# Second weights in two sets, four staging tiles, streamed token operands and PSUM banks by chain in a fused attention and mixture kernel

## The chip, the cores and the metric

The kernel runs on one core of one Trainium2 chip. The time is device microseconds of one execution. Below, PE is TensorE (matrix products), PEld its weight loads, DVE VectorE, ACT ScalarE, POOL GpSimd, and SP the SyncE queue, which issues every transfer of this kernel, in its own order.

## What is computed

First a linear attention with 4 batches, 8 heads, 576 rows and head size 64. Then its output, x of 2304 tokens by 512, goes through 8 experts. Every token visits every expert, and the weights P of the experts are balanced by eight rounds of normalising rows and columns.

```python
logits = x @ w_gate
P = np.exp(logits - logits.max())
for _ in range(8):
    P /= P.sum(1, keepdims=True) + 1e-09
    P /= P.sum(0, keepdims=True) + 1e-09
    P *= N / E
out = np.zeros((N, D), dtype=np.float32)
for e in range(E):
    h = np.maximum(x @ w1[e], 0.0)     # w1[e]: 512 x 1024
    ye = h @ w2[e]                     # w2[e]: 1024 x 512
    out += P[:, e:e + 1] * ye
```

## The kernel before

The attention takes the first 0.2 ms. The rest, some 1.45 ms, is the expert part, and the change lies there.

**Units and steps.** The work of the experts is cut into 16 units: 8 experts, each in two halves of 512 hidden columns (`units`). In each unit the 2304 tokens go by in three chunks of 768 (`CT`, `NCH`), and the second product of a unit is done in 9 steps of two token tiles each (`NP`, `steps`). A step `s` is a unit `u` and a place `n` from 0 to 8 in it. The scheduler that places the instructions of each engine works on a list of 144 steps. It may move an instruction ahead of its place in the program as far as its data and its buffers allow.

**Seven products for eight.** Both matrix products are cut into 2 x 2 blocks and done by seven block products, in the order `ORDER = [1, 5, 6, 3, 7, 2, 4]`, with sums of blocks on either side. Each operand is split into a high and a low part (`wh`, `wl` for weights; `ah`, `al`, `sh`, `sl`, `bh`, `bl` for the left side), and a block product is three products of parts, each in two pieces: six matmuls. `first(u, c, i, g)` does the first layer (banks `hx`, `hz`; 6 matmuls of 384 columns, 42 such groups in a unit), `second(s, i)` the second one (6 matmuls of 256 columns, 63 such groups in a unit). `left_operands_a` and `left_operands_b` make the left sides of a step on DVE and ACT.

**Chains of the second product.** The seven products of a step are summed in three PSUM banks that `bank(name)` hands out: chain x takes 1, 6, 7, 4, chain z takes 5 and 3, and w takes 2. After each product DVE adds the bank into the output tiles (line 660). The next product of the same chain writes on into the same bank, so PE waits at it until DVE has read. Before, x, z, w and the small matmuls of the balancing share four banks of one pool, and whichever is free is handed out.

**Weights.** `stage(u, w)` loads a weight block of a unit as two tiles `st` of 512 KB, out of three staging buffers. `split(u, w, i)` makes the operand of product i: POOL adds or subtracts blocks (line 193; for the second weights in place, in `st`), ACT casts the high part `wh` (line 223), DVE makes the low part `wl` (line 224). First weights have 7 buffers of each part, one set. Second weights have 7 + `W2X` = 11.

**Token operands.** The seven sums of token blocks of each chunk are made once, at the end of the attention, and written to DRAM (`xdram`). In each unit `load_next` brings them back into one of `XSB = 4` buffers `xs`, in the order of use, one load each time a buffer comes free. The operand of product 1 is an exception (`RES = (1,)`): it is loaded once for each chunk into a tile `xr` that stays.

Of the kernel before, what the change touches and what calls it, by code (L numbers as in the profile page):

```python
# [9 lines left out]
F32 = mybir.dt.float32  # L10
# [6 lines left out]
def raw(ap):  # L17

    return ap.bitcast(F32)
# [3 lines left out]
def moe_attention_kernel(  # L23
# [29 lines left out]
    P = 128  # L53
# [3 lines left out]
    SM = JM * P  # L57
    SR = S - SM
    XSB = 4
    RES = (1,)  # L60
    W2X = 4
    FB = 4
    NFB = FF // P // FB
    CT = 6
# [3 lines left out]
    HD = DM // 2  # L68
# [5 lines left out]
    wp = ctx.enter_context(tc.tile_pool(name="wp", bufs=1, side="right"))  # L74
    ps_cm = tc.tile_pool(name="ps", bufs=6, space=bass.MemoryType.PSUM)
    ps = [ps_cm.__enter__()]
    kv_cm = tc.tile_pool(name="ps_kv", bufs=2, space=bass.MemoryType.PSUM, side="right")
    ps_kv = kv_cm.__enter__()

    def bank(name):  # L80
        return ps[0].tile([P, 512], F32, tag="b", name=name)


    ident = const.tile([P, P], F32, name="ident")
# [4 lines left out]


    ORDER = [1, 5, 6, 3, 7, 2, 4]
    xdram = {}

    def token_tile():
# [2 lines left out]
    def token_operands(c, x):  # L97
# [11 lines left out]

        for i in ORDER:  # L110
            if i == 5:
# [61 lines left out]
    wst, wt = {}, {}  # L173
    tmp = {}

    def stage(u, w):
        e, fb = units[u]
        f0 = fb * FB * P
        for r in range(2):
            wst[u, w, r] = t = wp.tile([P, 2, 2, HD], F32, tag="st", bufs=3, name="st")  # L180
            if w == 1:
                src = w1[e][r * HD : (r + 1) * HD, f0 : f0 + FB * P]
            else:
                src = w2[e][f0 + r * HD : f0 + (r + 1) * HD, :]
            nc.sync.dma_start(out=t.rearrange("p k h c -> p k (h c)"), in_=src.rearrange("(k p) c -> p k c", p=P))

    def split(u, w, i):

        def q(r, h):
            return wst[u, w, r][:, :, 1 - h if w == 1 else h]  # L190

        def tt(o, a, b, op=ALU.subtract):
            nc.gpsimd.tensor_tensor(o, a, b, op=op)  # L193


        if w == 1:

            if i == 5:
                tmp[u] = wp.tile([P, 2, HD], F32, tag="t", bufs=1, name="t")
                tt(tmp[u], q(0, 1), q(1, 1), ALU.add)  # L200
            elif i == 6:
                tt(tmp[u], tmp[u], q(0, 0))
            elif i == 3:
                tt(tmp[u], q(1, 0), tmp[u])
            elif i == 7:
                tt(q(0, 1), q(0, 0), q(0, 1))
            o = {1: q(0, 0), 7: q(0, 1), 2: q(1, 0), 4: q(1, 1)}[i] if i not in (5, 6, 3) else tmp[u]
        else:

            if i == 5:  # L210
                tt(q(0, 0), q(0, 1), q(0, 0))
            elif i == 6:
                tt(q(0, 0), q(0, 0), q(1, 1))
            elif i == 7:
                tt(q(0, 1), q(1, 1), q(0, 1))
            elif i == 4:
                tt(q(0, 0), q(1, 0), q(0, 0), ALU.add)
            o = {3: q(1, 1), 7: q(0, 1), 2: q(1, 0)}.get(i, q(0, 0))
        pool = wp if w == 1 else op_
        bufs = 7 + W2X * (w == 2)  # L220
        hi = pool.tile([P, 2, HD], F32R, tag=f"w{w}h", bufs=bufs, name="wh")
        lo = pool.tile([P, 2, HD], F32R, tag=f"w{w}l", bufs=bufs, name="wl")
        nc.scalar.copy(hi, o)  # L223
        (nc.vector if u > 0 or (w == 2 and i in (1, 6, 7, 4)) else nc.gpsimd).tensor_tensor(lo, o, raw(hi), op=ALU.subtract)  # L224
        wt[u, w, i] = (hi, lo)
# [18 lines left out]
    for i in range(2):  # L244
        r, cl = slice(i * D, (i + 1) * D), slice(i * M, (i + 1) * M)
# [253 lines left out]


    outt = {}
    hp_, px, pz = [], [], []
    NP = CT // 2 * NCH
    steps = [(u, n) for u in range(len(units)) for n in range(NP)]
    def order(u):

        return [NCH - 1] + list(range(NCH - 1)) if u == 0 else list(range(NCH))

    chunks = [(u, c) for u in range(len(units)) for c in order(u)]
    hraw, hneg, ops, xop, xres, hacc = {}, {}, {}, {}, {}, {}  # L510
    loads = [(u, c, i) for u, c in chunks[1:] for i in ORDER]

    def load_next():

        while loads:
            u, c, i = loads.pop(0)
            if i in RES:
                if (c, i) not in xres:
                    xres[c, i] = op_.tile([P, 2, 2, HL], F32R, name=f"xr{c}_{i}")
                    nc.sync.dma_start(out=raw(xres[c, i]), in_=xdram[c, i])  # L520
                xop[u, c, i] = xres[c, i]
                continue
            xop[u, c, i] = token_tile()
            nc.sync.dma_start(out=raw(xop[u, c, i]), in_=xdram[c, i])
            return

    def first(u, c, i, g):
# [38 lines left out]
        if g == 1 or both is None:  # L566
# [5 lines left out]
            else:  # L572
                nc.scalar.copy(o, src)  # L573
        if g == 1 and (u, c) != chunks[0] and i not in RES:
            load_next()

    def tiles_of(u, n):

        c, j = order(u)[n // (CT // 2)], n % (CT // 2)
        return [CT * c + j, CT * c + j + CT // 2]  # L580
# [90 lines left out]

    pieces = [(u, c, i, g) for u, c in chunks for i in ORDER for g in range(2)]

# [56 lines left out]
    for i, jb in enumerate(jobs):  # L730
# [4 lines left out]
        if i >= 8 and i % 2 == 0 and (i - 8) // 2 < 7:  # L735
            split(0, 1, ORDER[(i - 8) // 2])
        if i == 24:
# [14 lines left out]
    left_operands_b(0)  # L752
    sc_cm.__exit__(None, None, None)
    ps_cm.__exit__(None, None, None)
    ps[0] = ctx.enter_context(tc.tile_pool(name="ps4", bufs=4, space=bass.MemoryType.PSUM))
    pz.append(ctx.enter_context(tc.tile_pool(name="pz", bufs=1, space=bass.MemoryType.PSUM)))
    op_ = ctx.enter_context(tc.tile_pool(name="op", bufs=1, reuse_waits="tile"))
    for _ in range(XSB):
        load_next()
    for i in ORDER:  # L760
        split(0, 2, i)
# [3 lines left out]
    for s, (u, n) in enumerate(steps):  # L765
        c = n // (CT // 2)
        more = u + 1 < len(units)
        if u == NFB:
            for t in tiles_of(u, n):
                nc.vector.tensor_scalar_mul(outt[t], outt[t], prob[:, t, 0:1])  # L770
        if more:
            if n == 1:
                stage(u + 1, 1)
            if n == 2:
                split(u + 1, 1, ORDER[0])
            if n == NP - 2 - W2X:
                stage(u + 1, 2)
            if NP - 1 - W2X <= n < NP - 1:
                split(u + 1, 2, ORDER[n - (NP - 1 - W2X)])
        for k, i in enumerate(ORDER):  # L780
            second(s, i)
            if n == NP - 1 and more and k + W2X < len(ORDER):
                split(u + 1, 2, ORDER[k + W2X])
            if k < (5, 5, 4)[n % 3] and todo:
                pc = todo.pop(0)
                first(*pc)
                j = ORDER.index(pc[2])
                if pc[1] == order(pc[0])[-1] and pc[3] == 1 and pc[0] + 1 < len(units) and j + 1 < len(ORDER):
                    split(pc[0] + 1, 1, ORDER[j + 1])
            if i == 7 and s + 1 < len(steps):  # L790
                left_operands_a(s + 1)
            if k in (1, 4):
                next(gate, None)
        if s + 1 < len(steps):
            left_operands_b(s + 1)
        if s == NFB * NP - 1:
            for _ in gate:
                pass
        if u == len(units) - 1:
            for t in tiles_of(u, n):  # L800
                store(t)
        ops.pop(s)
# [28 lines left out]
```

## Time and profile before

| | us |
|---|---|
| three runs, median (lowest, highest) | 1668.83 (1668.63, 1671.46) |
| profiled execution, its own time | 1676.44 |
| its span, first to last instruction | 1674.7 |
| PE busy in the span | 1626.8 |
| DVE busy | 1430.5 |
| ACT busy | 783.6 |
| POOL busy | 250.1 |

The profiled execution is 7.6 us longer than the median. PE is busy nearly throughout, but its matmuls overlap, and the end of each is modelled; how fast PE goes is seen from the starts of its instructions, not from the busy share. A wait of DVE, ACT or POOL costs nothing unless PE comes to need what it delays.

### The profile page before, as it was taken

The numbers are of one execution on the slowest core, as the hardware profiler recorded it, in microseconds if no ns is written. First come the engines' busy times: TensorE is split into PE (matmuls) and PEld (weight loads), VectorE is DVE, ScalarE is ACT, GpSimd is POOL, SyncE is SP. The second block draws the span as 40 slices with busy tenths as digits, with TensorE's granted clock in tenths as the row PEclk, the third lists the DMA queues.
The fourth block names the chain that finished last, engine by engine and source line by source line (L and its number), as shares of the span: only waits on it lengthen the run. The fifth ranks groups of instructions, "written<-read, shape, count | busy, mean of one in ns | idle before, by whom it ended". The sixth has DMA issues, their size and how long they took to land.

```text
span 1674.7 us, 29917 instructions
## 1 busy us (share of the span) xinstructions
PE 1626.8 (97%) x11610; PEld 1601.4 (96%) x11610; DVE 1430.5 (85%) x2903; ACT 783.6 (47%) x1408; POOL 250.1 (15%) x232
## 2 busy tenths in 40 slices
PE   7999989999999999999999999999999999999998
PEld 7899889999999999999999999999999999999997
DVE  7999788898978888898888887888889888888878
ACT  6777645443344344443444443434444344444432
POOL 7531131110111011010101010101101010101000
PEclk9999999999999999999999999999999999999999
DMA  9422575554554555556555454555564654555452
GB/s 242 119 80 99 218 284 190 196 194 159 169 177 159 195 175 176 195 162 209 177 175 188 163 187 163 176 189 183 166 206 157 205 185 162 189 159 194 159 189 76
DMA packets 96347, 295.08 MB, mean 176 GB/s; under 512 B 13776, under 2 KB 38352, under 8 KB 96208
## 3 DMA queue, kind: packets, MB, share of 16 engines
q1 hardware_dynamic: 96208, 293.19, 53.0%
q8 instruction: 92, 1.51, 0.4%
q14 instruction: 47, 0.39, 0.1%
HBM read 271.93 MB, written 21.23 MB: 175 GB/s over the span
## 4 chain that ended last, share of the span: by engine, by line
PE 73%; DVE 16%; DMA 5%; issue 2%; ACT 2%; POOL 1%; SPq 0%; ACTq 0%; DVEq 0%
PE hx L554 20%; PE x L640 19%; PE hz L554 13%; PE z L640 10%; DMA st<-in_moe_w_dram 5%; PE w L640 5%; DVE sm L591 3%; DVE wl L224 2%; DVE out L660 2%; DVE hr L571 1%; PE np L433 1%; DVE mx L347 1%; POOL st L193 1%; ACT wh L223 1%; DVE bl L591 1%
## 5 line engine op out<-in xcount | busy, mean ns | idle before, releaser
L554 PE MATMUL hx<-xs,wh 128*128 128x384 f32 x1160 | 279.9, 336 | 0.8 <-ACT hr L573 0.5
L554 PE MATMUL hz<-xs,wh 128*128 128x384 f32 x1152 | 278.3, 336 | 0.0
L660 DVE SCALAR_TENSOR_TENSOR out<-x,prob,out 128x256 f32<-128x256 f32 x504 | 237.8, 476 | 22.9 <-PE x L640 22.8
L554 PEld LDWEIGHTS hx<-xs,wh 128*128 128x128 f32 x1160 | 204.1, 188 | 1.4 <-ACT hr L573 0.9
L554 PEld LDWEIGHTS hz<-xs,wh 128*128 128x128 f32 x1152 | 203.2, 188 | 0.1
L622 ACT ACTIVATE bh<-hr 128x512 fp32r<-128x512 f32 x144 | 91.1, 633 | 233.0 <-PE x L640 188.1
L223 ACT CAST wh<-st 128x512 fp32r<-128x512 f32 x176 | 106.7, 618 | 194.9 <-POOL st L193 80.1
L224 DVE TENSOR_TENSOR wl<-st,wh 128x512 fp32r<-128x512 f32 x169 | 135.1, 802 | 67.2 <-ACT wh L223 66.3
L660 DVE SCALAR_TENSOR_TENSOR out<-z,prob,out 128x256 f32<-128x256 f32 x252 | 120.1, 476 | 83.2 <-PE z L640 83.0
L591 DVE SCALAR_TENSOR_TENSOR sm<-hr,sm 128x256 f32<-128x256 f32 x288 | 147.8, 513 | 3.9
L554 PE MATMUL hx<-xs,wl 128*128 128x384 f32 x580 | 150.8, 336 | 0.0
L554 PE MATMUL hz<-xs,wl 128*128 128x384 f32 x576 | 149.7, 335 | 0.0
L193 POOL TENSOR_TENSOR st<-st 128x512 f32<-128x512 f32 x80 | 106.7, 1342 | 231.1 <-DMA st<-in_moe_w_dram 177.0
L618 ACT CAST sh<-sm 128x512 fp32r<-128x512 f32 x144 | 89.6, 622 | 99.7 <-PE z L640 75.6
L640 PE MATMUL z<-wh,sh 128*128 128x256 f32 x576 | 117.4, 284 | 13.0 <-DVE out L660 12.2
L640 PE MATMUL x<-wh,sh 128*128 128x256 f32 x576 | 118.9, 288 | 2.7 <-ACT wh L223 1.3
L640 PE MATMUL z<-wl,sh 128*128 128x256 f32 x576 | 119.6, 282 | 0.8 <-POOL wl L224 0.8
L640 PE MATMUL x<-wl,sh 128*128 128x256 f32 x576 | 117.0, 281 | 0.0
L640 PE MATMUL z<-wh,sl 128*128 128x256 f32 x576 | 115.1, 281 | 1.8 <-DVE sl L606 1.8
L640 PE MATMUL x<-wh,sl 128*128 128x256 f32 x576 | 115.4, 281 | 0.0
L591 DVE SCALAR_TENSOR_TENSOR bl<-hr,bh 128x512 fp32r<-128x512 f32 x144 | 112.9, 784 | 0.0
L193 POOL TENSOR_TENSOR t<-st 128x512 f32<-128x512 f32 x16 | 21.2, 1322 | 608.4 <-DMA st<-in_moe_w_dram 527.3
(153 smaller groups left out, 3968.4 us busy)
## 6 DMA issues: line engine op xcount, KB each, us to landing
xs<-xd SPq DMA_DIRECT2D x282, 768.0 KB, 4.4
st<-in_moe_w_dram SPq DMA_DIRECT2D x64, 512.0 KB, 5.7
xd<-xs SPq DMA_DIRECT2D x21, 768.0 KB, 4.2
k<-in_k_dram SPq DMA_DIRECT2D x8, 512.0 KB, 6.7
v<-in_v_dram SPq DMA_DIRECT2D x8, 512.0 KB, 5.6
q<-in_q_dram SPq DMA_DIRECT2D x8, 512.0 KB, 6.5
out_dram<-out SPq DMA_DIRECT2D x16, 256.0 KB, 2.3
xr<-xd SPq DMA_DIRECT2D x3, 768.0 KB, 11.5
```

What stands on the lines that cost most here:

```text
L193: nc.gpsimd.tensor_tensor(o, a, b, op=op)
L223: nc.scalar.copy(hi, o)
L224: (nc.vector if u > 0 or (w == 2 and i in (1, 6, 7, 4)) else nc.gpsimd).tensor_tensor(lo, o, raw(hi), op=ALU.subtract)
L347: nc.vector.reduce_max(mx, p3, axis=AX.X)
L433: nc.tensor.matmul(n3[:, i, :], lhsT=qt[g][:, i, :], rhs=kvs[key[0]][:, h, :], start=True, stop=True)
L554: nc.tensor.matmul(pb, lhsT=a[:, k, g * P : (g + 1) * P], rhs=x[:, b, k, :], start=i in (1, 5, 2) and j == 0, stop=j == len(prods) - 1, sk ...
L571: nc.vector.tensor_tensor(o, src, o, op=ALU.add)
L591: nc.vector.scalar_tensor_tensor(o, in0=a, scalar=0.0, in1=b, op0=ALU.max, op1=op)
L618: nc.scalar.copy(sh, sm)
L622: nc.scalar.activation(bh, a[:, 1:], AF.Relu)
L640: nc.tensor.matmul(pb, lhsT=ops[s][i][a][:, f], rhs=wt[u, 2, i][b][:, f], start=bool(start) and j == 0, stop=j == len(prods) - 1, skip_gro ...
L660: nc.vector.scalar_tensor_tensor(o, in0=pb, scalar=prob[:, t, e : e + 1], in1=o, op0=ALU.mult, op1=ALU.add)
```

## The change

- `RES` becomes empty: the operand of product 1 is streamed like the other six, 21 loads of a unit where there were 18, and the three `xr` tiles and their loads are gone.
- The second weights have 14 buffers of each part, two sets (`bufs = 7 * w`). Both staging calls stand at the start of a unit (n = 1 and n = 2), and the seven splits of the second weights stand at places listed in `W2AT`.
- Four staging buffers `st` where there were three.
- Once the expert part has begun, `bank` gives chain x two banks of its own, z one, and w one, which it shares with the balancing. It is four banks as before.

```diff
-    RES = (1,)
-    W2X = 4
+    RES = ()
+    pz = []
     def bank(name):
-        return ps[0].tile([P, 512], F32, tag="b", name=name)
+        if not pz:
+            return ps[0].tile([P, 512], F32, tag="b", name=name)
+        tag = name if name in "xz" else "w"
+        return ps[0].tile([P, 512], F32, tag=tag, bufs=2 if tag == "x" else 1, name=name)
+    W2AT = [(5, 2), (6, 0), (6, 3), (7, 0), (7, 3), (8, 0), (8, 3)]
-            wst[u, w, r] = t = wp.tile([P, 2, 2, HD], F32, tag="st", bufs=3, name="st")
+            wst[u, w, r] = t = wp.tile([P, 2, 2, HD], F32, tag="st", bufs=4, name="st")
-        bufs = 7 + W2X * (w == 2)
+        bufs = 7 * w
-    hp_, px, pz = [], [], []
+    hp_, px = [], []
-    ps[0] = ctx.enter_context(tc.tile_pool(name="ps4", bufs=4, space=bass.MemoryType.PSUM))
+    ps[0] = ctx.enter_context(tc.tile_pool(name="ps4", bufs=1, space=bass.MemoryType.PSUM))
                 split(u + 1, 1, ORDER[0])
-            if n == NP - 2 - W2X:
+            if n == 2:
                 stage(u + 1, 2)
-            if NP - 1 - W2X <= n < NP - 1:
-                split(u + 1, 2, ORDER[n - (NP - 1 - W2X)])
         for k, i in enumerate(ORDER):
             second(s, i)
-            if n == NP - 1 and more and k + W2X < len(ORDER):
-                split(u + 1, 2, ORDER[k + W2X])
+            if more and (n, k) in W2AT:
+                split(u + 1, 2, ORDER[W2AT.index((n, k))])
```

What stands on the engines is set by the scheduler. Three places show it. The first is SP's queue. Before, in the middle of unit 5, it holds the second tile of the second weights for unit 6 (`st_8956`) and the first tile of the first weights for unit 7 (`st_9785`):

```order
L524 DMA xs_9098<-xd2_4_3079 128x1536
L524 DMA xs_9133<-xd0_5_1826 128x1536
L524 DMA xs_9167<-xd0_6_1908 128x1536
L185 DMA st_8956<-in_moe_w2_dram 128x2x512
L524 DMA xs_9244<-xd0_3_1986 128x1536
L524 DMA xs_9279<-xd0_7_2076 128x1536
L524 DMA xs_9388<-xd0_2_2158 128x1536
L185 DMA st_9785<-in_moe_w1_dram 128x2x512
L524 DMA xs_9458<-xd0_4_2238 128x1536
```

Now both tiles of the second weights for unit 6 (`st_8874`, `st_8876`) stand in the middle of unit 4:

```order
L532 DMA xs_8094<-xd0_1_1733 128x1536
L532 DMA xs_8128<-xd0_5_1826 128x1536
L193 DMA st_8874<-in_moe_w2_dram 128x2x512
L532 DMA xs_8200<-xd0_6_1908 128x1536
L532 DMA xs_8239<-xd0_3_1986 128x1536
L193 DMA st_8876<-in_moe_w2_dram 128x2x512
L532 DMA xs_8320<-xd0_7_2076 128x1536
```

So these loads moved ahead by a whole unit, and loads of operand 1 (`xd0_1`) came into the queue.

The second place is DVE, at the low parts of those weights. Before, in step 4 of unit 5, `wl_9326` and `wl_9440` (second weights for unit 6) stand among first weights (`wl_9170`, `wl_9247`), and ahead of the reads of chains x and z:

```order
L591 SCALAR_TENSOR_TENSOR sm_9177<-hr_8627,hn_8887 128x512
L571 TENSOR_TENSOR hr_8967<-hz_9222,hr_8967 128x2x3x128
L224 TENSOR_TENSOR wl_9170<-st_8730,wh_9169 128x512
L591 SCALAR_TENSOR_TENSOR sm_9198<-hr_8627,sm_9177 128x256
L224 TENSOR_TENSOR wl_9326<-st_8954,wh_9325 128x512
L660 SCALAR_TENSOR_TENSOR out9_3977<-x_8958,prob_79,out9_3977 128x256
L591 SCALAR_TENSOR_TENSOR sm_9198<-hr_8627,sm_9198 128x256
L224 TENSOR_TENSOR wl_9440<-st_8956,wh_9439 128x512
L660 SCALAR_TENSOR_TENSOR out10_4107<-z_9105,prob_79,out10_4107 128x256
L660 SCALAR_TENSOR_TENSOR out7_4106<-x_9083,prob_79,out7_4106 128x256
L591 SCALAR_TENSOR_TENSOR bl_9076<-hr_8627,bh_9075 128x512
```

Now the low parts for unit 6 stand around the change from unit 4 to unit 5, seven within two steps, four of them close together:

```order
L668 SCALAR_TENSOR_TENSOR out17_3434<-x_8527,prob_79,out17_3434 128x256
L614 TENSOR_TENSOR sl_8612<-sm_8610,sh_8611 128x512
L599 SCALAR_TENSOR_TENSOR sm_8722<-hr_8298,hn_8570 128x512
L232 TENSOR_TENSOR wl_9408<-st_8874,wh_9407 128x512
L232 TENSOR_TENSOR wl_9478<-st_8876,wh_9477 128x512
L232 TENSOR_TENSOR wl_9529<-st_8874,wh_9528 128x512
L599 SCALAR_TENSOR_TENSOR sm_8743<-hr_8298,sm_8722 128x256
L232 TENSOR_TENSOR wl_9599<-st_8876,wh_9598 128x512
L599 SCALAR_TENSOR_TENSOR sm_8743<-hr_8298,sm_8743 128x256
L668 SCALAR_TENSOR_TENSOR out17_3434<-x_8527,prob_79,out17_3434 128x256
L668 SCALAR_TENSOR_TENSOR out3_3556<-z_8658,prob_79,out3_3556 128x256
L668 SCALAR_TENSOR_TENSOR out0_3555<-x_8642,prob_79,out0_3555 128x256
```

They are now a whole unit ahead of their use, and no longer among the first weights.

The third place is PE, in steps 73 and 74 (unit 8). Before, four groups of the second product (w, x, z, x) stand between two groups of the first layer:

```order
L640 MATMUL w<-wh,bh 128x256 x2
L640 MATMUL w<-wl,bh 128x256 x2
L640 MATMUL x<-wh,ah 128x256 x2
L640 MATMUL z<-wh,sh_11889 128x256 x2
L640 MATMUL z<-wl,sh_11889 128x256 x2
L640 MATMUL z<-wh,sl_11890 128x256 x2
L640 MATMUL x<-wh,sh 128x256 x2
L640 MATMUL x<-wl,sh 128x256 x2
L640 MATMUL x<-wh,sl 128x256 x2
L640 MATMUL w<-wh,bl 128x256 x2
L640 MATMUL x<-wl,ah 128x256 x2
L640 MATMUL x<-wh,al 128x256 x2
```

Now these rows are the middle of ten groups of the second product in a row, with nothing of the first layer between them:

```order
L648 MATMUL x<-wh,ah 128x256 x2
L648 MATMUL x<-wl,ah 128x256 x2
L648 MATMUL x<-wh,al 128x256 x2
L648 MATMUL x<-wh,bh 128x256 x2
L648 MATMUL x<-wl,bh 128x256 x2
L648 MATMUL x<-wh,bl 128x256 x2
L648 MATMUL z<-wh,sh 128x256 x2
L648 MATMUL z<-wl,sh 128x256 x2
L648 MATMUL z<-wh,sl 128x256 x2
L648 MATMUL w<-wh,bh 128x256 x2
L648 MATMUL w<-wl,bh 128x256 x2
```

Such a run of ten stands in two of the sixteen units (8 and 13). Elsewhere the longest runs are 7 or 8 groups, before and now.

## Rows read from the trace of the kernel before

**Rows 1.** The page's first part: busy us (share of the span) and instructions

```profile
span 1674.7 us, 29917 instructions
...
PE 1626.8 (97%) x11610; PEld 1601.4 (96%) x11610; DVE 1430.5 (85%) x2903; ACT 783.6 (47%) x1408; POOL 250.1 (15%) x232
```

**Rows 2.** The chain that ended last, in time: start us, us, what

```profile
637.15 6.08 DMA st<-in_moe_w_dram
...
651.21 1.92 PE hx L554 x11
659.08 2.08 PE hx L554 x12
...
1558.91 1.92 PE hx L554 x11
```

**Rows 3.** Timeline, 610 to 640 us: start us, us, engine line op out<-in xcount

```profile
616.91 0.40 PE L640 MATMUL z<-wh,sh 128*128 128x256 f32 x2
...
617.38 0.40 PE L640 MATMUL z<-wh,sl 128*128 128x256 f32 x2
```

**Rows 4.** PE's waits, 230 to 1650 us: who for whom, us, times, longest

```profile
PE z L640 <- DVE out L660: 12.2, 12, 1.3
PE x L640 <- DVE out L660: 2.4, 5, 0.9
PE w L640 <- ACT bh L622: 1.8, 5, 0.8
PE w L640 <- DVE bl L591: 0.5, 1, 0.5
```

**Rows 5.** SP's waits, whole span: who waited for whom, us, times, longest

```profile
SPq L185 <- DVE wl L224: 96.3, 40, 10.3
```

**Rows 6.** Timeline of SP, 636 to 652 us

```profile
637.15 0.38 SPq L185 DMA_DIRECT2D st<-in_moe_w_dram  x1
```

**Rows 7.** Timeline of all engines, 643 to 650.5 us

```profile
643.31 2.55 POOL L193 TENSOR_TENSOR st<-st 128x512 f32<-128x512 f32 x2 [11.22 <-DMA st<-in_moe_w_dram]
...
644.63 1.15 ACT L223 CAST wh<-st 128x512 fp32r<-128x512 f32 x2 [3.58 <-POOL st L193]
...
645.28 1.12 DVE L224 TENSOR_TENSOR wl<-st,wh 128x512 fp32r<-128x512 f32 x1 [2.63 <-ACT wh L223]
...
646.48 1.29 POOL L193 TENSOR_TENSOR st<-st 128x512 f32<-128x512 f32 x1 [0.63 <-DVE wl L224]
...
646.72 1.33 DVE L591 SCALAR_TENSOR_TENSOR sm<-hr,sm 128x256 f32<-128x256 f32 x1
...
647.45 0.40 PE L640 MATMUL x<-wh,al 128*128 128x256 f32 x2
...
647.97 0.68 DVE L224 TENSOR_TENSOR wl<-st,wh 128x512 fp32r<-128x512 f32 x1
...
648.58 0.47 DVE L660 SCALAR_TENSOR_TENSOR out<-z,prob,out 128x256 f32<-128x256 f32 x1
648.97 0.47 DVE L660 SCALAR_TENSOR_TENSOR out<-x,prob,out 128x256 f32<-128x256 f32 x1
...
649.11 0.51 PE L640 MATMUL z<-wh,sh 128*128 128x256 f32 x2 [1.25 <-DVE out L660]
```

**Rows 8.** Timeline of PE, 738 to 741 us, one unit later

```profile
738.19 0.40 PE L640 MATMUL x<-wh,al 128*128 128x256 f32 x2
739.62 0.50 PE L640 MATMUL z<-wh,sh 128*128 128x256 f32 x2 [1.03 <-DVE out L660]
```

**Rows 9.** DVE groups, 420 to 1620 us (busy us, mean ns; idle before)

```profile
L591 DVE SCALAR_TENSOR_TENSOR sm<-hr,sm 128x256 f32<-128x256 f32 x238 | 121.0, 508 | 3.3
L224 DVE TENSOR_TENSOR wl<-st,wh 128x512 fp32r<-128x512 f32 x142 | 112.3, 791 | 61.3 <-ACT wh L223 60.9
```

**Rows 10.** Timeline of DVE, 690 to 700 us, at the change of units

```profile
693.91 1.34 DVE L224 TENSOR_TENSOR wl<-st,wh 128x512 fp32r<-128x512 f32 x1 [2.42 <-ACT wh L223]
```

**Rows 11.** Line 524, loads of token operands, 400 to 1600 us

```profile
DMA to landing us min/median/max: 4.0/4.4/7.1
```

**Rows 12.** One unit: PE, PEld, DVE, ACT, POOL busy, PEclk, DMA share, GB/s

```profile
649.00:740.00 91.00, 89.86 (x633) 89.26 (x634) 78.36 (x152) 39.15 (x65) 10.41 (x8) 1.00 0.55 181
```

## The prediction, made before the changed kernel ran

> **What bounds the kernel now.** I read the busy shares first, then the chain that ended last, PE's waits, the timeline around one of them, and SP's waits.
>
> PE is busy 97% of the span [rows 1]. That share hides gaps, so I go by starts. A pair of second-layer matmuls follows the one before it after 0.47 us, four matmuls, so 0.1175 us each [rows 3]. A group of twelve first-layer matmuls takes 2.08 us, 0.1733 us each [rows 2]. A unit has 63 x 6 = 378 of the first kind and 42 x 6 = 252 of the other: 378 x 0.1175 + 252 x 0.1733 = 44.4 + 43.7 = 88.1 us. The same group of the chain comes back ten units later, from 651.21 to 1558.91 [rows 2], so a unit takes 90.77 us. That is 2.7 us over its floor, at the full clock (1.00) [rows 12]. In about 13 units the change can thus win at most 13 x 2.7 = 35 us.
>
> The largest part of the 2.7 us is one event that comes back in each unit. PE waits 12 times, 12.2 us in all, at chain z for DVE's read of the bank [rows 4]. One of the waits, read backwards: PE should start z at 647.45 + 0.24 = 647.69 and starts at 649.11, 1.42 us late, because DVE reads the bank only at 648.58 [rows 7]. DVE was late because it had waited 2.63 us for ACT's `wh`, that for POOL, and POOL 11.22 us for the tile `st` [rows 7]. The load of that tile was issued at 637.15 [rows 6], since SP waits for a staging buffer until DVE has made a `wl`: 96.3 us in 40 waits [rows 5]. It took 6.08 us and is a piece of the chain itself [rows 2]. One unit later z starts at 739.62 instead of 738.43, 1.19 us late [rows 8]. The mean is 1.3, and with the slower restart of the matmuls I take 1.4 us for each of the 12.
>
> **The change part by part.**
>
> *Staging and two sets.* With four staging buffers and a second set, both tiles of second weights are loaded about a unit ahead of use, and the splits no longer follow right behind a load. The wait at `st` goes, and with it the wait of DVE: it idles 61.3 us at `wl` [rows 9]. Gain: 12 x 1.4 = 16.8 us. If only every second event goes, it is 8.4; more than 16.8 isn't in it.
>
> *The other waits of PE for DVE* at x and w are 2.4 + 0.5 = 2.9 us [rows 4]. The z waits cost 16.8 us where 12.2 are shown as idle, a ratio of 1.4, so these cost about 4 us. DVE comes free earlier by up to 61.3 / 13 = 4.7 us in each unit, so I take the 4 us as gained; bounds 0 and 7 (with ACT's 1.8 and what is not shown as waiting). What would be late next is `bh` from ACT, those 1.8 us, which I leave.
>
> *The burst.* The seven splits of second weights now come close together, around a change of units. That is the cost. Before, the same 14 splits of a unit were spread, so their sum on DVE doesn't change, only their density. DVE is busy 78.36 us in a unit of 91 [rows 12]; 14 low parts at 0.79 [rows 9] leave 78.4 - 11.1 = 67.3 for the rest, 15.0 in two of the nine steps. PE needs 2/9 x 88.1 = 19.6 us for two steps. A `wl` alone takes 0.68 us [rows 7]; four of the seven splits also have a POOL operation of 1.29 us, and beside one of these DVE is slower: `wl` 1.12 for 0.68, `sm` 1.33 [rows 7] for a mean of 0.508 [rows 9], so 0.44 and 0.82 lost, 0.63 in the mean. Seven `wl` in two steps: 7 x 0.68 + 4 x 0.63 = 7.3, and 15.0 + 7.3 = 22.3, which is 2.7 us more than PE needs. How much of that does PE feel? At the change of units DVE stands idle 2.42 us today [rows 10], and at x, which comes there, PE waits only 2.4 us in all units together [rows 4]; so some 2.4 us are free. What is left is 0.3 us per unit, +3.9 us. Ends: 0 (no slowing beside POOL: 19.8 us against 19.6), and 2.9 per unit (rival B).
>
> *Runs of ten second products* on PE come twice, with no first layer between them in which DVE could catch up. Before, none is longer than 8. Ends 0 and 1.0 us each (the mean of a z wait, 12.2 / 12 [rows 4]); I take 0.7, nearer to the upper end, since DVE must make operands and reads at PE's pace: +1.4 us.
>
> *Streaming operand 1.* Three loads more in a unit, 21 for 18; one each 88.1 / 21 = 4.2 us. With four buffers a load is issued about three operands ahead, 12.6 us, and lands after 4.4 us in the median and 7.1 at most [rows 11]. DMA is at 0.55 [rows 12]; three of 786 KB more on 181 GB/s x 91 us = 16.5 MB are a seventh, so 0.63. It is hidden by the work on the three operands ahead. A load is late only when SP holds it back over 12.6 - 7.1 = 5.5 us. Longest wait of SP for staging is 10.3 us [rows 5], and today no first-layer matmul waits for a load [rows 4]. Cost 0; the upper end is rival C.
>
> *Own banks.* The reads of x and z that PE waits for are late because DVE is late, not because a bank was handed to someone else: PE's waits at x and z name DVE's read alone [rows 4]. In the order of the instructions x took turns on two banks before, too. I take 0, bounds -2 and +2: z on one bank must wait for its read, but between two products of z there are others of x or w, and each of these takes 6 x 0.1175 = 0.7 us on PE, against a read of 0.47 [rows 7].
>
> *The start.* The three resident loads go, the first streamed ones come, and there is a second set to fill. Within 2 us of nothing.
>
> Sum: -16.8 - 4 + 3.9 + 1.4 = -15.5 us. On the profiled execution that is 1676.4 - 15.5 = 1660.9. The median of the runs is 7.6 us below that execution, so the same change on it gives 1668.8 - 15.5 = 1653.3; I say **1653 us**. The best that the terms allow is -16.8 - 7 - 2 - 2 = -28, 1641; the worst is -8.4 + 3.9 + 2 + 2 = 0, which runs into rival A.
>
> **The rivals.**
>
> *A, no change.* The burst is just dense enough to put a stall of about the old size in the old one's place: 1.4 us per unit instead of 0.3. Then it is -16.8 - 4 + 13 x 1.4 + 1.4 = -1.2, **1668 us**. For it: 0.63 us lost beside each POOL operation is a mean of two rows, and at 0.9 us DVE would be 3.8 us behind, 1.4 after the 2.4 that are free. Against: the splits have a unit of time before they are needed, so the scheduler can let a read of a bank go ahead of them.
>
> *B, slower.* POOL holds DVE for the whole of each of its four operations: 7 x 0.68 + 4 x 1.29 = 9.9, and 15.0 + 9.9 = 24.9 us against 19.6; 5.3 late, less the 2.4 free, 2.9 per unit. Sum -16.8 - 4 + 13 x 2.9 + 1.4 = +18, **1687 us**. The place is the change of units, PE waiting at z or x for DVE's read. It decides from 0.9 us lost per operation on (rival A is that point). For it: `sm` at 646.72 lost 0.82 us [rows 7]. Against: `wl` at 645.28 lost only 0.44, and a POOL operation can also fall beside a DVE read of PSUM, of which the rows show no slowing (0.47 at 648.58 as at 648.97).
>
> The rows show DVE and POOL in each other's way in part. The Trainium skill (page "SBUF — State Buffer", section "🔬 SBUF: two separate sides") states a harsher rule that speaks against this change: the two share a pair of ports as an exclusive lock, so that a DVE instruction with two SBUF inputs and a GpSimd instruction that reads SBUF block each other for a whole instruction. By that rule each of the four POOL operations could cost DVE its full length, which is the time of this rival. The trace agrees that there is blocking (1.12 against 0.68 us) but in neither row for the whole 1.29 us.
>
> *C, operand 1 comes late.* SP waits 10.3 us for a staging buffer ahead of a token load, 4.8 over the 5.5 that are free. If that falls on one load in half of the units, it costs 6.5 x 4.8 = 31 us, which is -15.5 + 31 = +16, **1684**; on one or two units it is 1658 to 1663. For it: four buffers hold SP less, but both stagings now stand side by side early in a unit. Against: in the order, the loads of second weights moved to where a buffer is free long before.
>
> *D, the banks or buffers do nothing* and only the staging counts: that is the forecast already.
>
> **How the numbers follow.** About 0.2%, 3.3 us, can be told from no change. The forecast (1641 to 1665) has 0.66, A (1665 to 1672) 0.15, B 0.12, C 0.07, of which 0.03 is its mild form and still faster. Faster is 0.66 + 0.03 = 0.69, no change 0.15, slower 0.12 + 0.04 = 0.16. The range 1640 to 1671 holds the forecast, A and the mild form of C, 0.84, less a little beyond the ends.
>
> **What would show it.** Right: PE's z waits for DVE's read, 12.2 us, fall below 3; DVE's idle time at `wl` falls from 61.3 us to under 15; SP's waits for staging no longer end at a late load; a unit takes about 89.6 us. The burst: at each change of units a dense stretch of seven `wl` in about two steps, with a PE wait of about 0.3 us behind it; a wait of 1.4 there is A, of 2.9 is B. Streaming: hx waits for `xs` show C. The forecast is wrong if PE's period stays at 90.8 with z waits gone, or if z waits stay with DVE busy rather than idle ahead of them.

## The result and the profile after

| | us |
|---|---|
| before, six runs, median (lowest, highest) | 1671.66 (1668.63, 1673.56) |
| after, six runs, median (lowest, highest) | 1656.32 (1654.24, 1658.25) |
| ratio, with its 95% interval | 0.991 [0.9901, 0.992] |
| profiled execution of before, of after | 1676.44, 1655.71 |

The changed kernel is 15.3 us faster; 15.5 was forecast. As a time, 1653 us was forecast, from the median of 1668.83 us that three runs of before had; over six runs it is 1671.66, and the changed kernel stands 3 us above its forecast. The profiled executions differ by 20.7 us, since the one of before lies 4.8 us above the median of its kernel and the one of after 0.6 below.

First the page of after, span and busy time, which answers to [rows 1]:

```profile
span 1653.9 us, 30102 instructions
...
PE 1618.8 (98%) x11610; PEld 1600.7 (97%) x11610; DVE 1432.8 (87%) x2903; ACT 785.7 (48%) x1408; POOL 277.4 (17%) x232
```

PE, DVE, ACT and POOL have as many instructions as they had, in a span 20.8 us shorter. POOL alone is busy 27 us longer: an operation on `st` takes 1661 ns in the mean where it took 1342. PE's waits from 230 to 1630 us (who for whom, us in total, times, longest) answer to [rows 4]:

```profile
PE w L648 <- DVE bl L599: 1.9, 7, 0.4
PE w L648 <- DVE out L668: 1.3, 3, 0.4
PE w L648 <- ACT bh L630: 0.8, 3, 0.3
PE x L648 <- DVE out L668: 0.7, 4, 0.2
```

The 12 waits of chain z, 12.2 us, are gone; no wait of z is left in this window. The groups of DVE from 420 to 1600 us (busy us, mean ns; idle before) answer to [rows 9]:

```profile
L599 DVE SCALAR_TENSOR_TENSOR sm<-hr,sm 128x256 f32<-128x256 f32 x239 | 113.4, 475 | 2.3
L232 DVE TENSOR_TENSOR wl<-st,wh 128x512 fp32r<-128x512 f32 x138 | 97.5, 718 | 6.1 <-ACT wh L231 5.8
```

DVE idles 6.1 us at the low parts of weights where it idled 61.3. The chain that ended last (start us, us, what) holds the same group of the first layer ten units apart, as [rows 2] did:

```profile
503.27 2.08 PE hx L562 x12
...
1397.34 2.09 PE hx L562 x12
```

(1397.34 - 503.27) / 10 = 89.4 us for a unit; it was 90.77, and 89.6 was forecast. The loads of `st`, pieces of some 6 us of this chain before [rows 2], are no part of it any more: POOL waited 13 times for such a load before it could split second weights, and in the changed kernel not once (420 to 1600 us). SP's waits for a staging buffer answer to [rows 5]:

```profile
SPq L193 <- DVE wl L232: 107.3, 45, 4.5
```

Their sum did not fall (96.3 us before), only the longest of them, from 10.3 to 4.5 us. So the sum doesn't tell whether a load comes late.

The seven splits of second weights do come close together around the change of units. POOL from 676 to 690 us in the changed kernel (timeline; start us, us, engine, line, out<-in):

```profile
676.33 3.11 POOL L201 TENSOR_TENSOR st<-st 128x512 f32<-128x512 f32 x2 [43.30 <-DVE wl L232]
681.19 1.29 POOL L201 TENSOR_TENSOR st<-st 128x512 f32<-128x512 f32 x1 [1.75 <-DVE wl L232]
686.04 3.55 POOL L201 TENSOR_TENSOR st<-st 128x512 f32<-128x512 f32 x1 [3.55 <-DVE wl L232]
```

and the low parts on DVE in the same place (its other operations left out):

```profile
675.57 0.68 DVE L232 TENSOR_TENSOR wl<-st,wh 128x512 fp32r<-128x512 f32 x1
680.44 0.67 DVE L232 TENSOR_TENSOR wl<-st,wh 128x512 fp32r<-128x512 f32 x1
685.28 1.89 DVE L232 TENSOR_TENSOR wl<-st,wh 128x512 fp32r<-128x512 f32 x3
687.42 0.68 DVE L232 TENSOR_TENSOR wl<-st,wh 128x512 fp32r<-128x512 f32 x1
690.28 0.69 DVE L232 TENSOR_TENSOR wl<-st,wh 128x512 fp32r<-128x512 f32 x1
```

Seven in 15.4 us, about one and a half steps, so as dense as I assumed. DVE is held there beside POOL:

```profile
676.90 1.39 DVE L599 SCALAR_TENSOR_TENSOR bl<-hr,bh 128x512 fp32r<-128x512 f32 x1
678.22 1.51 DVE L599 SCALAR_TENSOR_TENSOR sm<-hr,sm 128x256 f32<-128x256 f32 x1
...
681.82 0.95 DVE L599 SCALAR_TENSOR_TENSOR al<-hr,ah 128x256 fp32r<-128x256 f32 x1
```

Alone, such a `bl`, `sm` and `al` take 0.68, 0.41 and 0.41 us (as at 689.54, 687.09 and 693.02), so 2.35 us are lost. DVE has idled 2.82 us just before this stretch, and from 671.82 to 699.7 us it never idles. Between 670 and 700 us PE waits for nothing that the profile shows. At the same place PE waits some 0.35 us for `bl` in three of the twelve units from 420 to 1600 us (at 501.9, 948.9 and 1396.0).

What is new stands in the runs of second products. Here DVE and PE around 976 us, at the end of such a run (unit 8):

```profile
974.68 1.39 DVE L627 TENSOR_TENSOR sl<-sm,sh 128x512 fp32r<-128x512 f32 x1
...
975.99 0.47 DVE L668 SCALAR_TENSOR_TENSOR out<-w,prob,out 128x256 f32<-128x256 f32 x1
...
976.62 0.47 PE L648 MATMUL w<-wh,bh 128*128 128x256 f32 x2 [0.42 <-DVE out L668]
...
977.52 0.50 PE L648 MATMUL x<-wh,sh 128*128 128x256 f32 x2 [0.19 <-DVE out L668]
```

PE waits twice. By starts the two cost 0.58 and 0.35 us, 0.9 together. The same pair stands at 529.61 and 1423.67, five units to either side, so three times in all. Each time the `sl` ahead of the read takes 1.39 us instead of 0.68, beside a POOL operation (here one of 1.68 us from 973.85), so POOL's hold on DVE is a part of this event. And the count of such runs, given ahead of the prediction as two in the changed kernel and none before, is wrong: in the traces ten groups stand in a row three times in the changed kernel (from 524.8, 971.8 and 1418.8 us) and twice in the kernel before (from 403.1 and 496.3 us).

### The profile page after: what moved, and what is told of

It reads as the page before. It is cut to its first block, busy times and chain, and to the rows that moved or that the text cites. A ratio compares the mean times of both kernels' runs of the same rounds, so it can differ in the third digit from the quotient of the medians.

```text
span 1653.9 us, 30102 instructions
## 1 busy us (share of the span) xinstructions
PE 1618.8 (98%) x11610; PEld 1600.7 (97%) x11610; DVE 1432.8 (87%) x2903; ACT 785.7 (48%) x1408; POOL 277.4 (17%) x232
## 4 chain that ended last, share of the span: by engine, by line
PE 88%; DVE 9%; ACT 1%; issue 1%; DMA 0%; POOL 0%; SPq 0%; ACTq 0%; DVEq 0%
PE hx L562 24%; PE x L648 23%; PE hz L562 18%; PE z L648 11%; PE w L648 6%; PE np L441 1%; DVE out L668 1%; DVE mx L355 1%; DVE sm L599 1%; PE kv L371 1%; PE pp L349 1%; PE qp L418 1%; DVE cn L358 1%; DVE cn L357 1%; DVE bl L599 1%; PE pp L350 1%
## 5 line engine op out<-in xcount | busy, mean ns | idle before, releaser
L562 PE MATMUL hx<-xs,wh 128*128 128x384 f32 x1536 | 372.6, 336 | 0.3 <-DVE prob L169 0.3
L562 PEld LDWEIGHTS hx<-xs,wh 128*128 128x128 f32 x1536 | 270.1, 188 | 0.6 <-issue 0.5
L201 POOL TENSOR_TENSOR st<-st 128x512 f32<-128x512 f32 x80 | 132.9, 1661 | 704.6 <-DVE wl L232 656.1
L562 PE MATMUL hx<-xs,wl 128*128 128x384 f32 x768 | 199.3, 336 | 0.0
L626 ACT CAST sh<-sm 128x512 fp32r<-128x512 f32 x144 | 89.6, 622 | 131.2 <-PE z L648 97.4
L599 DVE SCALAR_TENSOR_TENSOR sm<-hr,sm 128x256 f32<-128x256 f32 x288 | 136.7, 475 | 2.8
L562 PEld LDWEIGHTS hx<-xs,wl 128*128 128x128 f32 x768 | 138.9, 188 | 0.0
L232 DVE TENSOR_TENSOR wl<-st,wh 128x512 fp32r<-128x512 f32 x169 | 120.9, 727 | 8.1 <-ACT wh L231 7.6
L607 ACT ACTIVATE ah<-hr 128x256 fp32r<-128x256 f32 x144 | 60.4, 419 | 138.5 <-PE x L648 118.2
```

Of the source, the lines that this page charges most:

```text
L562: nc.tensor.matmul(pb, lhsT=a[:, k, g * P : (g + 1) * P], rhs=x[:, b, k, :], start=i in (1, 5, 2) and j == 0, stop=j == len(prods) - 1, sk ...
L599: nc.vector.scalar_tensor_tensor(o, in0=a, scalar=0.0, in1=b, op0=ALU.max, op1=op)
L607: nc.scalar.activation(ah, a11, AF.Relu)
L626: nc.scalar.copy(sh, sm)
```

## The experiments

The change has four parts: streaming, the fourth staging buffer, the second set with its early places, and the banks. My theory was that the late load is the stall, and that the fourth buffer together with the second set takes it off the path; streaming and banks are worth nothing.

**Streaming alone.**

```diff
-    RES = (1,)
+    RES = ()
```

> The kernel before with one edit: operand 1 is streamed (RES empty). Theory (the loads of second weights that wait for a staging buffer are the stall, streaming is hidden): 1671.7 within 3 us, z waits of PE near 12 us in some 12 events as before, no first-layer matmul waits for a load. Rival (streamed operands come late, or streaming itself helps by shortening SP's queue of waits): a change over 3 us either way, with waits of hx for xs, or with fewer z waits.

Measured: 1671.71 against 1672.20, ratio 1.0001 [0.9991, 1.0012]. The 12 waits of z are there as before, and no first-layer matmul waits for a load:

```profile
PE z L640 <- DVE out L660: 7.4, 12, 1.3
PE x L640 <- DVE out L660: 1.7, 5, 0.5
```

Streaming costs and gives nothing. What it does is make room: the three resident tiles took 6 KB of each partition each, a staging tile takes 4 KB, and before, less than 4 KB of a partition were free. These rows show one thing more. The z waits sum to 7.4 us in this execution against 12.2 [rows 4], with their count the same and the median time the same, so [rows 4] is a large one. The two profiled executions differ by 4.7 us, about as much as these waits; whether the execution or the changed order makes them smaller isn't shown.

**Streaming and the fourth buffer.**

```diff
-    RES = (1,)
+    RES = ()
-            wst[u, w, r] = t = wp.tile([P, 2, 2, HD], F32, tag="st", bufs=3, name="st")
+            wst[u, w, r] = t = wp.tile([P, 2, 2, HD], F32, tag="st", bufs=4, name="st")
```

> The kernel before with operand 1 streamed and four staging buffers, second weights still in 11 buffers and at their old places, shared banks. Theory (the staging buffer alone sets the late load): z waits fall from 12.2 us to under 3, DVE's idle time at wl from 61 us to under 20, and the time falls by 12 to 18 us to about 1656. Rival (the second set is what takes the splits off the path): the splits still come just ahead of use, the loads come early but the time falls by less than 5 us, to 1667 or more.

Measured: 1657.92, ratio 0.9909 [0.9895, 0.9923], 13.8 us below streaming alone. PE's waits, all of z for DVE's read gone:

```profile
PE w L640 <- ACT bh L622: 3.6, 13, 0.5
PE x L640 <- DVE out L658: 1.5, 2, 0.9
PE w L640 <- DVE bl L591: 1.4, 5, 0.3
```

and POOL's waits for loads, of this kernel:

```profile
POOL t L193 <- DMA st<-in_moe_w_dram: 193.3, 10, 20.0
POOL st L193 <- DMA st<-in_moe_w_dram: 109.8, 3, 36.9
```

against those of the kernel before:

```profile
POOL t L193 <- DMA st<-in_moe_w_dram: 478.2, 11, 45.1
POOL st L193 <- DMA st<-in_moe_w_dram: 153.0, 13, 15.1
```

The splits of second weights (`st`) waited for their load in each unit, 13 times, and now 3 times. So one buffer of 512 KB takes the whole gain, without a second set, with the splits at their old places and with shared banks.

**The changed kernel with three staging buffers**, the same line set back from 4 to 3:

> The changed kernel with three staging buffers again; two sets, streaming and own banks stay. Theory (the fourth buffer is needed): SP waits for a buffer again, a wl waits for a late load, z waits come back to 8 to 12 us and the time to 1667 to 1673. Rival (with a whole set ahead a late load does not matter, since its split is not needed for a unit): within 3 us of the changed kernel, 1656.

Measured: 1702.90, ratio 1.0177 [1.0158, 1.0196]: 46 us slower than the changed kernel and 31 slower than before. The late load came back, as expected: from 420 to 1600 us POOL waits for it 13 times, 162.2 us in all. But its price was far over what I gave, and it is paid at x more than at z (20.5 and 4.2 us of PE's waits for DVE's read). Either the early places or the second set makes it so much worse.

**The second set, old places, three staging buffers.**

```diff
-    RES = (1,)
+    RES = ()
-        bufs = 7 + W2X * (w == 2)
+        bufs = 7 * w
```

> The kernel before with operand 1 streamed and 14 buffers of second weights, but three staging buffers and the splits and stagings at their old places in the program; differs from the slow three-buffer kernel (1703) in those places and in the banks. If the second set alone lets DVE queue up low parts in front of a late load, it is slow too: 1685 or more, with x or z waits of over 1 us behind a wl. If the early places of splits and stagings do it, it is near the streamed kernel of before: 1672 within 5 us.

Measured: 1697.52, ratio 1.0152 [1.0132, 1.0173]. Three buffers of weights more than streaming alone, and nothing else, cost 26 us. One event in the timeline, from the issue of the load to PE:

```profile
819.53 0.39 SPq L185 DMA_DIRECT2D st<-in_moe_w_dram  x1
```

```profile
824.89 2.54 POOL L193 TENSOR_TENSOR st<-st 128x512 f32<-128x512 f32 x2 [13.70 <-DMA st<-in_moe_w_dram]
...
826.87 1.11 DVE L224 TENSOR_TENSOR wl<-st,wh 128x512 fp32r<-128x512 f32 x1 [2.65 <-ACT wh L223]
...
828.29 1.61 DVE L224 TENSOR_TENSOR wl<-st,wh 128x512 fp32r<-128x512 f32 x1
...
831.74 0.51 PE L640 MATMUL x<-wh,sh 128*128 128x256 f32 x2 [0.41 <-DVE out L660]
...
832.21 1.28 DVE L224 TENSOR_TENSOR wl<-st,wh 128x512 fp32r<-128x512 f32 x2
...
834.35 0.68 DVE L224 TENSOR_TENSOR wl<-st,wh 128x512 fp32r<-128x512 f32 x1
834.95 0.47 DVE L660 SCALAR_TENSOR_TENSOR out<-x,prob,out 128x256 f32<-128x256 f32 x1
...
835.48 0.51 PE L640 MATMUL x<-wh,ah 128*128 128x256 f32 x2 [2.05 <-DVE out L660]
```

With room for a whole second set the scheduler puts five low parts on DVE within some 8 us, among reads and left operands, all behind the one that waits for the load. When it is late they all are, and so is the read of x behind them: DVE idles 2.65 us, makes the five, and PE waits first 0.41 and then 2.05 us. That with 11 buffers fewer of them can stand there is argued, not looked up. This event stands twice in the trace (PE at 835.48 and 1297.74); other waits at x and z are shorter, some of them behind a DVE operation that POOL holds, so it isn't the whole of the 26 us. What is shown is that the second set is no help against a late load, and that the kernel with it is much slower.

**The banks.** The changed kernel with the shared banks of before:

> The changed kernel with the four PSUM banks of before, shared by all chains. Theory (own banks are worth nothing): 1656 within 3 us, the waits of PE at x, z and w together within 2 us of the changed kernel's 5. Rival (own banks remove waits of chains for each other's banks): 1660 or more, with waits of x, z or w for a read of another chain.

Measured: 1657.24, ratio 0.9904 [0.9888, 0.9919]; the changed kernel again gave 1656.41 (below). No difference; PE's waits at x, z and w are 5.8 us. And the kernel before with own banks as its one edit:

> The kernel before with own PSUM banks for chains x, z and w as the one edit. Theory: no change, 1671.7 within 3 us, z waits near 12 events as before. Rival (z on one bank must wait more often for its read while DVE is late): 3 us or more slower, more z events.

Measured: 1668.57, ratio 0.9982 [0.997, 0.9994], 12 z waits of 9.2 us in all. That is 1.6 us by medians, within the 3 us expected, though the interval leaves out 1.

**The low parts of second weights on POOL.**

```diff
-        (nc.vector if u > 0 or (w == 2 and i in (1, 6, 7, 4)) else nc.gpsimd).tensor_tensor(lo, o, raw(hi), op=ALU.subtract)
+        (nc.vector if (u > 0 and w == 1) or (u == 0 and w == 2 and i in (1, 6, 7, 4)) else nc.gpsimd).tensor_tensor(lo, o, raw(hi), op=ALU.subtract)
```

> The changed kernel with the low parts of all second weights (from unit 1 on) made by POOL in place of DVE: it takes 7 x 0.72 = 5.0 us per unit off DVE and puts 7 of about 1.3 us on POOL, which read SBUF. Theory (POOL slows DVE in part, 0.63 us beside each such operation, and the burst has some price): 7 x 0.63 = 4.4 us come back on DVE, spread over the unit; 1656 within 4 us. Rival (POOL holds DVE for its whole operation): 9 us per unit for 5.0 taken off, DVE's two-input operations longer by over 1 us each time, 10 us or more slower. Rival (no contention to speak of): 3 to 8 us faster, DVE busy less by 5 us in a unit.

Measured: 1675.12, 18.7 us slower than the changed kernel's 1656.41. The groups of DVE show where the 5.0 us that were taken off it came back:

```profile
L599 DVE SCALAR_TENSOR_TENSOR sm<-hr,sm 128x256 f32<-128x256 f32 x235 | 161.1, 686 | 3.6
...
L599 DVE SCALAR_TENSOR_TENSOR sm<-hr,hn 128x512 f32<-128x512 f32 x118 | 94.7, 803 | 0.0
```

In the changed kernel the first takes 475 ns and the second 683. With 18 and 9 of them in a unit that is 18 x 0.211 + 9 x 0.120 = 4.9 us, 0.70 us for each of the seven POOL operations. So DVE got nothing; its busy time even rose, from 1432.8 to 1445.8 us. The loss of 18.7 us isn't in that sum but in its place:

```profile
595.08 2.77 POOL L201 TENSOR_TENSOR st<-st 128x512 f32<-128x512 f32 x2
595.21 2.93 DVE L599 SCALAR_TENSOR_TENSOR sm<-hr,sm 128x256 f32<-128x256 f32 x2
...
598.06 0.47 DVE L668 SCALAR_TENSOR_TENSOR out<-x,prob,out 128x256 f32<-128x256 f32 x1
...
598.59 0.51 PE L648 MATMUL x<-wh,ah 128*128 128x256 f32 x2 [1.34 <-DVE out L668]
```

Two operations of POOL, one right behind the other, hold two `sm` of DVE, one each: 2.93 us for some 0.8. The read of x stands behind them, and PE waits 1.34 us, 12 times, 16.1 us in all; the same two POOL operations stand ahead of each of the 12. That is the mechanism of rival B, a DVE operation held until POOL is done, in a kernel that has the POOL work for it. Its size is not the one that rival B gave (1.29 us, each POOL operation lost in full): DVE loses only what is left of the operation under way, in the mean 0.70 us, near the 0.63 of the theory. So the theory had the sum nearly right and the time wrong, and the rival the time right and the sum wrong.

The prediction held against rival B that a read of a bank isn't slowed, from the reads at 648.58 and 648.97 [rows 7]. That reading was empty, since POOL's last operation there ends at 646.48 + 1.29 = 647.77. A row of this kernel shows it:

```profile
593.18 1.82 POOL L232 TENSOR_TENSOR wl<-st,wh 128x512 fp32r<-128x512 f32 x1 [40.95 <-ACT wh L231]
...
593.76 0.48 DVE L668 SCALAR_TENSOR_TENSOR out<-x,prob,out 128x256 f32<-128x256 f32 x1
```

**Three buffers for streamed operands**, `XSB` 3 in place of 4 in the kernel with streaming and the fourth staging buffer:

> The kernel before with operand 1 streamed and four staging buffers (1657.9), with three buffers for streamed operands in place of four. Theory (four buffers have 12.6 us ahead against landings of 4.4 to 7.1, so streaming is hidden with room of one buffer): two operands ahead are 8.4 us, still over 7.1, so 0 to 5 us slower, 1658 to 1663, with a few first-layer waits for xs. Rival (the room with four was nearly used up): 15 us or more slower, waits for xs in each unit.

Measured: 1654.59, ratio 0.9904 [0.9889, 0.9919], no slower than with four (0.9909). Its waits for loads are seen, and small:

```profile
PE hz L554 <- DMA xs<-xd: 3.5, 10, 1.4
```

So with one buffer fewer the waits begin, too small to lengthen the time: four buffers had room of one, and rival C (operand 1 late) did not come with three either.

**The changed kernel again, and three kernels beside it on the same chip.**

> The changed kernel itself once more, beside the next three on one chip, so that they can be compared with it in small numbers. 1656 within 3 us.

Measured: 1656.41, ratio 0.9903 [0.989, 0.9916].

The kernel with streaming and the fourth buffer, with 13 buffers of second weights (`W2X` 6) in place of 11:

> The kernel before with operand 1 streamed, four staging buffers and 13 buffers of second weights (W2X 6), the splits two steps earlier each. Between the kernel with 11 (1657.9) and the changed one with 14. Theory: 1657 within 3 us. Rival (each buffer more buys something): 2 us or more below 1657.9. Rival (early splits are a burden where four staging buffers must hold the blocks longer): 3 us or more above, with z or x waits behind a wl.

Measured: 1658.33, ratio 0.9913 [0.9901, 0.9925]. With shared banks, 11, 13 and 14 buffers of second weights give 1657.92, 1658.33 and 1657.24: once four staging buffers are there, the set's size decides nothing.

The kernel with streaming and the fourth buffer, with own banks:

> The kernel before with operand 1 streamed, four staging buffers and own banks; second weights in 11 buffers at their old places. It lacks the second set and the early places alone. Theory (second set and early places are worth nothing once no load is late): the changed kernel's time within 3 us, 1653 to 1659. Rival (a set ahead is worth something of its own): over 3 us slower than the changed kernel, with low parts of weights behind which reads of x or z wait.

Measured: 1670.20, ratio 0.9992 [0.9981, 1.0002]. That is outside the theory's 1653 to 1659, and the rival's size without the rival's cause. Nearly the whole gain over before is gone, though the waits of z for its bank are gone too. What stands there instead is POOL:

```profile
647.07 1.36 POOL L200 TENSOR_TENSOR t<-st 128x512 f32<-128x512 f32 x1 [18.41 <-DMA st<-in_moe_w_dram]
647.32 2.84 DVE L598 SCALAR_TENSOR_TENSOR sm<-hr,sm 128x256 f32<-128x256 f32 x2
...
648.51 1.36 POOL L200 TENSOR_TENSOR st<-st 128x512 f32<-128x512 f32 x1
...
650.08 0.47 DVE L667 SCALAR_TENSOR_TENSOR out<-x,prob,out 128x256 f32<-128x256 f32 x1
...
650.61 0.51 PE L647 MATMUL x<-wh,ah 128*128 128x256 f32 x2 [0.81 <-DVE out L667]
```

It is again two POOL operations in a row, the first of them for first weights (`t`), and two `sm`, the second held until POOL's second ends (647.32 + 2.84 = 650.16, and 648.51 + 1.36 = 649.87). PE's waits at x for DVE's read are 12.3 us in all, 15 times. Ten of them are over 0.3 us, 11.3 us together, and ahead of each stands a DVE operation that POOL holds in this way. The same pair of POOL operations is in the kernel with shared banks too (at 734.04 and 735.41), and there DVE is held as well (`bl` takes 1.39 us), but no read that PE wants next stands behind it, and PE waits 0.22 us for `bl`. So the banks cost nothing as banks; the edit moved the order of the instructions, and a pair of POOL operations fell in front of a read. Why the scheduler places it so with one bank assignment and not with the other I haven't followed. Read the other way, the second set with its early places is worth 13.8 us beside own banks (1670.20 and 1656.41) and nothing beside shared ones (1657.92 and 1657.24), so the parts do not simply add. That the fourth buffer, and not a lucky order, is the gain with shared banks rests on the traces and on the number of kernels: with four staging buffers five of them, the changed one included, lie between 1654.6 and 1658.3 us.

Six staging buffers with streaming, the set of 11 and shared banks:

> The kernel before with operand 1 streamed and six staging buffers. Theory (with the fourth buffer the load is in time, and time beyond that is not needed): 1657.9 within 3 us, SP's waits for staging below the 61.7 us of four buffers. Rival (part of the loads is still late with four, seen in 22.6 us of idle DVE at wl): 3 to 8 us faster, idle time at wl under 10 us.

Measured: **1645.21**, ratio 0.984 [0.9827, 0.9852]: 27 us faster than before, 11 faster than the changed kernel. The rival's direction held, by more than it gave; SP's waits for staging, expected below 61.7 us, were 79.3. DVE's low parts of weights:

```profile
L224 DVE TENSOR_TENSOR wl<-st,wh 128x512 fp32r<-128x512 f32 x141 | 97.3, 698 | 7.5 <-ACT wh L223 7.5
```

DVE idles 7.5 us there, where four buffers left 22.6 and three 61.3. POOL waits for no load, and no kind of wait of PE comes to more than 1.0 us in all; with four buffers PE waited 3.6 us at w for ACT's `bh`, and here 0.8. By the starts of the matmuls, against the steps of 0.1175 and 0.1733 us that the prediction used, it stands 10.9 us over its floor in 13 units; the kernel with four buffers 19.4, the changed kernel 16.4, and before 36.5. That the earlier loads are the whole of this second gain is not shown: the changed kernel and the one with 13 buffers idle as little at the low parts (6.1 and 5.1 us) and take 1656.4 and 1658.3 us. The Trainium skill (page "Perfetto Trace Analysis", section "Optimization Strategy") says that a gap which repeats on the engine that should be busy can mean that there is no room for the next tile; these runs agree, with 1671.7, 1657.9 and 1645.2 us at three, four and six buffers.

## Why the prediction was right, and where not

*The stall and its cause* were right. The reading back from z's wait to `wl`, `wh`, POOL, the load and SP's wait for a buffer [rows 4 to 7] is what the fourth buffer alone undoes. By the starts of the matmuls, z's reads cost 15.3 us in the profiled execution of before and 0.6 in that of after: 14.7 gained where 16.8 was the term.

*The part named for it* was wrong in half. I put the gain down to staging and two sets together. With shared banks the second set gives nothing beside four staging buffers (1657.2 and 1657.9), and it costs 26 us with three. "The splits no longer follow right behind a load" came from the buffer.

*Other waits of PE for DVE*: 4 us was the term. At x, by starts, 10.8 us became 3.4, and at w those for `bl` went from 2.0 to 3.8. So about 5.6 gained, within the bounds of 0 and 7. ACT's `bh` at w, which I left, gave 1.9.

*The burst*: +3.9 was the term, the small rest of two sizes near each other, 2.7 us more work than PE's time allows and 2.4 us free. By the rows at 676.90 to 681.82 POOL's four operations cost DVE 2.35 us (4 x 0.63 = 2.5 was taken), and DVE idled 2.82 us just before, so nothing is left over in most units; in three PE is late for `bl`, 1.8 us in all by starts, which are counted above under `bl`. The price was right, but the reading behind it was wrong. I took 0.44 and 0.82 us as what a DVE operation loses beside POOL, and said that neither row shows a whole block. But `wl` of [rows 7] starts at 645.28, while POOL's pair ends at 643.31 + 2.55 = 645.86; 0.58 us of rest and 0.68 of its own work, overlapped a little, make its 1.12. It lost all of the rest that there was to lose. The Trainium skill (page "SBUF — State Buffer", section "🔬 SBUF: two separate sides") says that of a DVE instruction with two SBUF inputs and a GpSimd instruction that reads SBUF the one that starts first blocks the other for the whole instruction; these rows and the 2.93 and 2.84 us for some 0.8 above agree with it, and my weighing against it was wrong. What such a hold costs in time is not DVE's loss but whether a read that PE needs stands right behind. In the changed kernel none does at most changes of units, so rival B's mechanism is real and its place was rarely hit.

*Runs of ten*: +1.4 for two; it is three events (units 3, 8 and 13) of 0.9 us, 2.8 us. The prediction's comparison, that none is longer than 8 before, rests on the miscount; what the rows show in each event is an `sl` held by POOL. About 1.0 of the 2.8 us is counted at x above too.

*Streaming* at nothing was right (1.0001), with one token buffer to spare. *Own banks* at nothing was right in the changed kernel, and as a general statement wrong: alone they moved it by 0.2%, and beside the fourth buffer by 12 us, through the order.

*The sum*: on the profiled execution -15.5 was forecast and -20.7 came. The burst's 3.9 that didn't come as such, 1.9 at `bh` and 1.6 more at x and w make most of the 5 us, against 2.1 less at z. On the medians it was -15.3. The profiled execution of before had larger z events than two other kernels with the same 12 events (12.2 us, against 9.2 and 7.4) and lies 4.8 us above its median, so the median agrees with the forecast to 0.2 us partly by luck: two errors cancel.

## What to carry to other kernels

Where the busiest engine waits once in each round, follow the wait back over every engine to the buffer that the first of them lacked, and give it that buffer alone: here 512 KB of staging were worth 14 us, and two more buffers another 13. More buffers further down, behind the late load, can let a scheduler queue more work behind it: here three of them cost 26 us. When an edit is worth nothing by its own mechanism, its change of the order can still be worth as much as the rest, so the place where two POOL operations meet a DVE operation that reads two operands from SBUF is looked up after each edit.

## What the runs showed of the hardware

A DVE operation with two SBUF operands that meets a POOL operation ends after it: two `sm`, beside two POOL operations in a row, took 2.84 and 2.93 us where they take some 0.8 alone, and ended 0.29 us after POOL's second in both cases. It goes the other way too: in the changed kernel a POOL operation at 686.04 took 3.55 us where 1.29 is its time alone, while DVE made `wl` and `sm` without a break until 688.43. A read of a bank while POOL worked (at 593.76 in the kernel with low parts on POOL) took 0.48 us, as it does otherwise. Seven low parts moved from DVE to POOL, 5.0 us per unit, cost DVE 4.9 us of such holding back, and POOL needed 1.59 us for each in the mean where 1.29 is its time alone.
